# First product with w_out summed for four units at once in two of the ring's PSUM banks

## The chip, the cores and the metric

The kernel runs on one core of a Trainium2 chip. A core has TensorE for matrix products, VectorE, ScalarE and GpSimd for elementwise work, and SyncE, which issues most of the transfers. Every engine works through its own queue in order. The metric is the device time of one execution in microseconds; the median of three runs is compared. Matrix products write to PSUM, which has eight banks; everything else lies in SBUF.

## The reference: delta rule attention, then a gated feed-forward layer

For each of 4 batches x 8 heads, with 768 positions of 48 features, a state matrix is carried along the sequence:

```
k_n = k / (norm(k) + 1e-6)
for t in range(S):
    y[t] = q[t] @ state
    v_old = kn[t] @ state
    state += b[t] * outer(kn[t], v[t] - v_old)
```

The results, 3072 rows of 384 features, go through `h = x @ w_in` (384 x 2048), `g = h * sigmoid(1.702 h)` and `g @ w_out` (2048 x 384). All products are in 32-bit floats. The two weight matrices come as 64-bit floats and are converted on the chip.

## The kernel before

**Units.** The sequence is cut into 6 chunks of 128 positions. A unit is one chunk of one batch, so there are 24 units, four per chunk; two neighbouring units share a column block of x^T (`xT`, 256 tokens). Inside a unit the recurrence becomes a triangular system, solved in four blocks of 32 positions: `solve` multiplies by a block's inverse (into `psU`), `below` takes the solved block out of the later ones (into `psR`), `solved` copies psU on ScalarE, `rest` subtracts psR from V on VectorE. `scores` makes psQ (queries against keys and state, in two halves of two banks each), `queries` and `outputs` make psY (outputs) and the new state.

**Steps.** `woven(n, share)` is one step of the main part, from n = 3 on. It works on unit n-1 (its last blocks and its output), n and n+1 together, in three stages; in each it calls `together` (psU and psR) and then hands out pieces of the feed-forward layer with `spend`, so that TensorE has something to do while other engines evacuate. A step gets a share of 13.0 us for n up to 6 and 20.8 after that. `STEPS` tells how many operations of the next inversion (`invert`, VectorE) each stage gets; two steps share an inversion, begun at the odd one (5, 7, ...).

**The queue.** `queue` holds generators; each yield is a piece of 1.3 us. `hidden` makes gelu(x @ w_in) (tiles `gT`), `written` makes g @ w_out of two units, one after the other. For the first chunk's first two units stands `both_written`, which goes feature block by feature block (16 blocks f of 128 features, in the list `order`) and adds up both units in the two banks of ps_moe; the two other units follow by `written`. `follow` appends the next pair's two generators in every second step. What is left at the end runs without cover.

**Weights.** `fetch_in` and `fetch_out` bring raw 64-bit words, `conversion` turns them into 32-bit floats by five operations on VectorE and one on ScalarE. `conversions` puts the pieces in a row, so that a `fill(k)` anywhere issues the next k substeps; five substeps make one piece. w_out's raw words lie partly in rows of w_out that are not yet converted (`inside`: the first row) and partly in borrowed buffers (`outside`: the name of the borrowed tile). `fetches` tells which transfer is started when a piece is done. Transfers of the first eight entries of `order` go by GpSimd's queue, the others by SyncE's.

**Order.** Operations that go through `vec`, `act`, `pe`, `pool`, `sync` and `other_queue` keep the order in which the program issues them on their engine (their line is the helper's, 102); a plain `nc.sync.dma_start` may be moved by the scheduler (lines 87, 95, 554, 724, 768).

**Buffers.** PSUM: ps_big 2 banks, ps_seq 4 ("the ring": psU, psR, half of psQ, psY), ps_moe 2 (ph, po). In SBUF the tag gT has 8 buffers, which `spare` also lends to other uses; the tags M, xT have 3, and `o` (the rows of the result, and `last`, a part of the outputs that two units share) has 2.

**Keys.** `normalize_mixed` scales a unit's keys: the square on ScalarE, the sum on VectorE, the power on GpSimd, then reciprocal and product on VectorE. A step calls it for a later unit.

Of the kernel before, what the change touches and what calls it, by code (L numbers as in the profile page):

```python
# [8 lines left out]
F32 = mybir.dt.float32  # L9
I32 = mybir.dt.int32  # L10
# [4 lines left out]
PSUM = bass.MemoryType.PSUM  # L15
# [3 lines left out]
def kernel(  # L19
# [21 lines left out]
    B, H, S, D = q.shape  # L41
    DM, DFF = moe_w_in.shape
    C = 128
    NC = S // C
    NBH = B * H
    NP = H // 2
    DP = 64
    KC = DM // 128
    FC = DFF // 128
    BS = 32  # L50
    NB = C // BS
    HB = 2
    NTH = HB * C
    FQ = 4
# [12 lines left out]
    io = ctx.enter_context(tc.tile_pool(name="io", bufs=3))  # L67
    wk = ctx.enter_context(tc.tile_pool(name="wk", bufs=2))
    ps_big = ctx.enter_context(tc.tile_pool(name="ps_big", bufs=2, space=PSUM))
    ps_seq = ctx.enter_context(tc.tile_pool(name="ps_seq", bufs=4, space=PSUM))  # L70
    ps_moe = ctx.enter_context(tc.tile_pool(name="ps_moe", bufs=2, space=PSUM))
    dram = ctx.enter_context(tc.tile_pool(name="dram", bufs=2, space=bass.MemoryType.DRAM))

# [10 lines left out]
    def load(n, pairs, dma=nc.sync.dma_start):  # L84
        c, b = units[n]
        for dst, src in pairs:
            dma(  # L87
                out=dst[n % len(dst)][:, :, 0:D],
                in_=src[b, :, c * C : (c + 1) * C, :].rearrange("h p d -> p h d"),
            )  # L90
# [9 lines left out]
    def pinned(op):  # L100

        return lambda *a, **kw: tc.keep_in_program_order(op(*a, **kw))  # L102

    class Engine:

# [75 lines left out]
                )  # L181

    places, slots = {}, {}
    inside = {3: 6, 4: 8, 5: 10, 6: 12, 7: 14, 12: 14, 13: 10}
    outside = {0: "xT", 8: "xT", 11: "xT", 1: "M", 9: "M", 14: "M", 2: "M2", 10: "M2", 15: "M2"}
    order = [0, 1, 2, 3, 4, 5, 6, 7, 8, 13, 9, 10, 12, 11, 14, 15]

    def fetch_out(f):

        if f in outside:  # L190
            slot = outside[f]
            if slot not in slots:
                slots[slot] = wk.tile([128, 2 * DM], I32, tag=slot[:2].strip("2"), name="raw", bufs=3)
            words = slots[slot]
        else:
            words = raws[:, inside[f] * DM : (inside[f] + 2) * DM]
        places[f] = as_raw(words, (1, DM))
        first = order.index(f) < FC // 2
        (other_queue if first else sync)(
            out=as_rows(places[f])[:, 0], in_=moe_w_out[f * 128 : (f + 1) * 128, :]  # L200
        )
# [51 lines left out]
    def conversions():  # L253
# [27 lines left out]
    fetches = {  # L281
        ("in", 0, 1): lambda: fetch_in(3),
        ("in", 3, 1): lambda: fetch_out(3),
        ("out", 4): lambda: fetch_out(13),
        ("out", 6): lambda: fetch_out(12),
    }
    for new, old in ((8, 0), (9, 1), (10, 2), (11, 8), (14, 9), (15, 10)):
        fetches[("out", old)] = lambda f=new: fetch_out(f)
    converting = conversions()

    def fill(n):
        for _ in range(n):
            next(converting, None)
# [142 lines left out]
    def spare(name):  # L436
        t = wk.tile([128, FQ, NTH], F32, tag="gT", name=name, bufs=GB)
        return t.rearrange("p f t -> p (f t)")
# [118 lines left out]


    def bank(name, shape=(128, H, D)):
        return ps_seq.tile(list(shape), F32, tag="seq", name=name)  # L560

    lasts = [None]

    class Step:
# [19 lines left out]
        def scores(self):  # L584

            c, S = self.c, slice(128, 128 + D)
            self.QS = (
                spare("QS")[:, 0 : NP * (128 + D)].rearrange("p (j t) -> p j t", j=NP) if self.n == B - 1
                else wk.tile([128, NP, 128 + D], F32, tag="QS", name="QS", bufs=3)
            )  # L590
            transposed(self.qp, self.QS[:, :, 0:128])
            if c > 0:
                St = ST[:, self.b, 0 : NP * D].rearrange("p (j d) -> p j d", j=NP)
                act.activation(self.QS[:, :, S], St, ACT.Copy)
            yield
            self.M = (
                spare("M").rearrange("p (h t) -> p h t", h=H) if self.n in (B - 1, B + 1)
                else wk.tile([128, H, 128], F32, tag="M", name="M", bufs=3)
            )
            n = 128 + D if c > 0 else 128  # L600
            for g in range(0, NP, 2):
                pool_, tag = (ps_seq, "seq") if g else (ps_big, "big")
                ps = [pool_.tile([128, 2, 128 + D], F32, tag=tag, name="psQ") for _ in range(2)]
                for i in range(2):
                    for hh in range(2):
                        r = self.rows(hh)
                        pe.matmul(
                            ps[hh][:, i, 0:n], lhsT=self.kT[r, g + i, :],
                            rhs=self.QS[r, g + i, 0:n], start=True, stop=True,
                        )  # L610
                for hh in range(2):
                    hs = slice(2 * g + hh, 2 * g + 4, 2)
                    if c > 0:
                        Vh = self.V[:, hs, :]
                        vec.tensor_tensor(Vh, Vh, ps[hh][:, :, S], op=ALU.subtract)
                    copy = act.copy if hh == 0 or self.n < 2 * B + HB else vec.tensor_copy
                    copy(self.M[:, hs, :], ps[hh][:, :, 0:128])
                if g == 0:
                    yield
            if self.n >= B:  # L620
                self.select()
# [146 lines left out]
            nc.sync.dma_start(out=out[b * S + c * C : b * S + (c + 1) * C, :], in_=o)  # L768
            yield 1.3

    def both_written(c, gT):

        po = [ps_moe.tile([128, DM], F32, tag="moe", name="po") for _ in range(HB)]
        for n, f in enumerate(order):
            ahead = order[min(n + 3, FC - 1)]
            while ("out", ahead - ahead % 2 if 4 <= ahead < 8 else ahead) not in done:
                fill(1)
            for i in range(HB):
                pe.matmul(
                    po[i], lhsT=gT[f // FQ][:, f % FQ, i * C : (i + 1) * C], rhs=w_out[:, f, :],  # L780
                    start=(n == 0), stop=(n == FC - 1),
                )
            if n < FC - 1:
                yield 1.3
        for i in range(HB):
            o = wk.tile([128, DM], F32, tag="o", name="o")
            act.copy(o, po[i])
            sync(out=out[i * S + c * C : i * S + (c + 1) * C, :], in_=o)
        yield 1.3
# [15 lines left out]
    def ahead_of(work, n):  # L805
        for _ in range(n):
            next(work, None)
# [57 lines left out]
            debt[0] -= done  # L865

    STEPS = (9, 5, 3, 3, 3, 3)
    begun = {}

    def woven(n, share):  # L870

        nonlocal inverting
        A, B_, D_ = steps.pop(n - 1, None), steps.get(n), steps.get(n + 1) or NoStep()
        m = n + B + 1
        if n < B + HB:
            K = normalize_mixed(m + 1) if n <= B else iter(())
        else:  # L880
            K = (normalize if n > 6 else normalize_mixed)(m) if m < len(units) else iter(())
        P = prepare(m) if m < len(units) else iter(())
        if m in begun:
            P = begun.pop(m)
        if n % HB == 1 and B < n and n + 1 + HB < len(units):
            inverting = invert(*units[n + 1 + HB], HB)
        ahead = STEPS[:3] if n % HB == 1 else STEPS[3:]

        next(K, None)
        together([(B_, 1)], [(A, 2)])  # L890
        run(D_.scored)
        next(K, None)
        ahead_of(inverting, ahead[0])
        spend(share / 3)

        together([(A, 3), (D_, 0)], [(B_, 1)])
        next(K, None)
        ahead_of(inverting, ahead[1])
        spend(share / 6)
        next(P, None)  # L900
        spend(share / 6)

        together([(B_, 2)], [(D_, 0)])
        if A:
            A.queries()
            A.outputs()
        run(P)
        ahead_of(inverting, ahead[2])
        if n % HB == 0:
            run(inverting)  # L910
        spend(share / 6)
        next(new_step(n + 2).scored, None)
        spend(share / 6)
        follow(n)
# [38 lines left out]
    late_U = room[:, 0 : H * D + XR]  # L953
    pool.memset(late_U[:, H * D :], 0.0)
    zs = room[:, 512 : 512 + 6 * B * H].rearrange("p (s b h) -> p s b h", s=6, b=B)
    psD = [ps_seq.tile([128, B, NP, BS], F32, tag="seq", name="psD") for _ in range(2)]
    warm(NW)
    for b in range(B):
        squares_first(b)
# [133 lines left out]
    load(B + 2, ((QP, q),), sync)  # L1093
    for n in range(2 * B + 1, 2 * B + 1 + HB):
        load(n, ((KN, k),), sync)
    for i in range(22):
        ahead_of(inverting, 1)
        if i < 18:
            feed()
        if i in (2, 3, 4, 7, 8, 9, 10):  # L1100
            fetch_out(i - 2 if i < 5 else i - 3)
    run(inverting)
    def beside_conversion(work):
        for cost in work:
            fill(2)
            yield cost

    queue = [beside_conversion(w) for w in ffn] + [both_written(0, gTs[0]), written(*units[HB], gTs[1])]
    for n in range(B - 1, len(units) + 1):
        woven(n, 20.8 if n > 6 else 13.0)  # L1110
    run(take(1e9))
# [31 lines left out]
```

## Time and profile before

| | before |
|---|---|
| median of 3 runs | 772.58 us (771.7 to 773.25) |
| the profiled execution | 771.55 us, of that 769.8 us span |
| mean granted clock of TensorE | 0.977 |
| TensorE po matmuls | 768, 263.4 us busy |
| TensorE ph matmuls | 1152, 261.2 us busy |
| VectorE busy | 439.8 us |
| output rows: issue to landing | 2.0 us, median of 24 |
| w_out raw words on SyncE, issue to landing | 3.1 and 3.4 us |

"Busy" is time in which an engine executes an instruction. A matmul row counts one instruction; a product of 32-bit floats takes two of them. The number after "idle before" is what the engine waited ahead of the instruction, with the one whose end released it. The granted clock is the share of full speed that TensorE was given. Transfers are listed by their issue; when they land is listed apart.

### The profile page before, as it was taken

What the parts mean: (1) busy time and instruction counts of PE and PEld (TensorE: products, weight loads), DVE (VectorE), ACT (ScalarE), POOL (GpSimd) and SP (SyncE); (2) the same over time, 40 slices, a digit from 0 to 9 for tenths busy, and PEclk for the clock granted to TensorE, in tenths of its full rate; (3) what the DMA queues carried; (4) which work ended last, traced back from release to release, by engine and by line L of the source; (5) the groups of instructions that cost most, each with busy time, mean ns of one, the idle gap of its engine ahead of it and who ended that gap; (6) DMA issues with size and microseconds to landing.
All of it is one profiled execution on the core that took longest, in us unless ns stands there. A gap on an engine that the chain in (4) does not pass through costs nothing.

```text
span 769.8 us, 19471 instructions
## 1 busy us (share of the span) xinstructions
PE 743.6 (97%) x8508; PEld 558.0 (72%) x8508; DVE 439.8 (57%) x896; ACT 240.1 (31%) x535; POOL 128.4 (17%) x133
## 2 busy tenths in 40 slices
PE   7888999888999999999999999999999999999997
PEld 6666788556687687687688678678678677686774
DVE  5999897996766566566566566565566521000000
ACT  4567523343233233133133133124123132121110
POOL 6133301100222122122131121220210000000000
PEclk8599999989999999999999999999999999999999
DMA  9965355543142142142142142142030020000000
GB/s 158 173 121 114 86 146 124 141 107 82 40 96 57 37 93 56 37 95 56 35 96 57 34 97 56 25 107 57 22 81 9 24 42 2 17 11 1 26 1 21
DMA packets 131637, 50.78 MB, mean 66 GB/s; under 512 B 106432, under 2 KB 127040, under 8 KB 131552
## 3 DMA queue, kind: packets, MB, share of 16 engines
q1 hardware_dynamic: 129152, 41.27, 24.9%
q0 software_dynamic: 2400, 8.26, 4.4%
q8 instruction: 67, 1.10, 0.6%
q14 instruction: 18, 0.15, 0.1%
HBM read 32.08 MB, written 16.25 MB: 63 GB/s over the span
## 4 chain that ended last, share of the span: by engine, by line
PE 83%; DVE 8%; SPq 4%; issue 1%; ACT 1%; DMA 1%; POOL 0%; DVEq 0%; ACTq 0%
PE ph L102 32%; PE po L102 30%; PE psY L102 6%; PE psU L102 5%; SPq L102 4%; PE psQ L102 3%; PE psR L102 3%; PE psG L102 2%; DVE w_out L102 2%; PE psT L102 2%; DVE tmp L102 2%; DVE P L102 1%; DVE V L102 1%; DVE w_in L102 1%; DMA w_out<-in_moe_w_in_dram 1%
## 5 line engine op out<-in xcount | busy, mean ns | idle before, releaser
L102 PE MATMUL po<-w_out,gT 128*128 128x384 f32 x768 | 263.4, 494 | 3.3 <-DVE w_out L102 3.3
L102 PE MATMUL ph<-xT,w_in 128*128 128x256 f32 x1152 | 261.2, 383 | 0.3
L102 PEld LDWEIGHTS ph<-xT,w_in 128*128 128x128 f32 x1152 | 214.8, 190 | 32.5 <-issue 1.7
L102 PEld LDWEIGHTS po<-w_out,gT 128*128 128x128 f32 x768 | 142.2, 191 | 96.3 <-DVE w_out L102 4.2
L102 DVE TENSOR_TENSOR V<-V,psR 128x384 f32<-128x384 f32 (+2 forms) x72 | 40.1, 557 | 191.6 <-PE psR L102 191.0
L102 ACT ACTIVATE gT<-ph 128x512 f32<-128x512 f32 x96 | 56.5, 596 | 150.8 <-PE ph L102 150.7
L102 DVE TENSOR_TENSOR P<-NT,YB 64x8 f32<-64x8 f32 (+26 forms) x178 | 85.2, 479 | 4.7
L102 ACT COPY US<-psU 32x384 f32<-32x384 f32 x92 | 43.2, 470 | 139.6 <-PE psR L102 75.5
L102 PEld LDWEIGHTS psU<-V,XB 32*32 32x32 f32 x1536 | 58.3, 104 | 35.8 <-issue 25.6
L102 DVE TENSOR_REDUCE YB<-P 64x4 f32<-64x8 f32 (+27 forms) x178 | 77.2, 434 | 6.3 <-DVE P L102 0.2
L102 PE MATMUL psU<-V,XB 32*32 32x48 f32 x1536 | 69.5, 203 | 4.0 <-DVE V L102 3.9
L102 PE MATMUL psR<-US,G 32*32 32x48 f32 x2576 | 62.9, 204 | 1.0 <-issue 0.5
L624 POOL TENSOR_SCALAR_AFFINE_SELECT M<-M 128x1024 f32<-128x1024 f32 x20 | 25.1, 1253 | 220.9 <-DVE M L102 160.1
L102 PEld LDWEIGHTS psR<-US,G 32*32 32x32 f32 x2576 | 53.4, 104 | 2.0 <-issue 1.0
L102 PE MATMUL psQ<-QS,kT 48*128 48x176 f32 (+1 forms) x384 | 39.1, 350 | 5.4 <-ACT QS L102 5.4
L102 PEld LDWEIGHTS psQ<-QS,kT 48*128 48x128 f32 x384 | 32.1, 215 | 9.0 <-ACT QS L102 7.2
L102 DVE TENSOR_TENSOR P<-NT 64x256 f32<-64x256 f32 (+7 forms) x44 | 36.3, 825 | 0.3
L102 DVE TENSOR_REDUCE NT<-P 64x64 f32<-64x1024 f32 (+7 forms) x44 | 35.4, 803 | 1.5
L102 PE MATMUL psG<-kT 48*128 48x128 f32 x384 | 32.1, 304 | 1.9 <-ACT G L102 1.2
L102 ACT COPY o<-po 128x384 f32<-128x384 f32 x24 | 11.5, 479 | 71.5 <-issue 41.0
L87 POOL DMA_DIRECT2D KN<-in_k_dram x13 | 12.4, 953 | 116.1 <-PE psY L102 107.0
L102 ACT COPY M<-psQ 128x256 f32<-128x256 f32 x68 | 22.9, 377 | 24.8 <-DVE V L102 17.5
(102 smaller groups left out, 609.7 us busy)
## 6 DMA issues: line engine op xcount, KB each, us to landing
Nd<-G SPq DMA_DIRECT2D x16, 512.0 KB, 3.5
QP<-in_q_dram SPq DMA_DIRECT2D x24, 192.0 KB, 3.9
V<-in_v_dram SPq DMA_DIRECT2D x24, 192.0 KB, 3.3
out_dram<-o SPq DMA_DIRECT2D x24, 192.0 KB, 2.0
KN<-in_k_dram POOLq DMA_DIRECT2D x14, 192.0 KB, 3.8
NT<-Nd SPq DMA_DIRECT2D x20, 128.0 KB, 2.6
Yd<-YS SPq DMA_DIRECT2D x20, 128.0 KB, 2.5
XB<-Yd SPq DMA_DIRECT2D x20, 128.0 KB, 3.0
```

The costliest lines, as they stand in the source:

```text
L87: dma(out=dst[n % len(dst)][:, :, 0:D], in_=src[b, :, c * C : (c + 1) * C, :].rearrange("h p d -> p h d"),)
L102: return lambda *a, **kw: tc.keep_in_program_order(op(*a, **kw))
L624: (pool if self.n < B else nc.gpsimd).affine_select(out=self.M, in_=self.M, compare_op=ALU.is_gt, fill=0.0, base=0, pattern=[[0, H], [1, 1 ...
```

## The change

Four things are edited.

- `both_written` becomes `all_written`: the first chunk's four units are summed feature block by feature block. Two units stay in ps_moe's banks, two take two of the ring's four banks; the ring is split into two pools of two banks, and while the sums last (`turns[1]`) `seq` gives out only the first pool. Each half of a feature block is a piece, followed by 2 or 3 conversion substeps. The four output rows are copied out one after the other at the end and sent with the ordered `sync`.
- `order`, `inside`, `outside` and `fetches`: w_out's blocks come in another order, and the last parts' raw words lie elsewhere; blocks 9 and 11 use two gT buffers, fetched after block 7 has been multiplied. Unit 5's M goes to the pool M instead of a gT buffer.
- `SOON` replaces `STEPS` up to step 6: the inversion of steps 5 and 6 gets (0, 4, 6) and (5, 5, 5) operations in place of (9, 5, 3) and (3, 3, 3).
- Key 9's square is issued ahead of the main part, at turn 14 of the loop before it, and `beside_conversion` issues 3 substeps per piece in place of 2 once w_in is converted.

```diff
--- before.py
+++ after.py
@@ -67,7 +67,7 @@
     io = ctx.enter_context(tc.tile_pool(name="io", bufs=3))
     wk = ctx.enter_context(tc.tile_pool(name="wk", bufs=2))
     ps_big = ctx.enter_context(tc.tile_pool(name="ps_big", bufs=2, space=PSUM))
-    ps_seq = ctx.enter_context(tc.tile_pool(name="ps_seq", bufs=4, space=PSUM))
+    ps_seq = [ctx.enter_context(tc.tile_pool(name=f"ps_seq{i}", bufs=2, space=PSUM)) for i in range(2)]
     ps_moe = ctx.enter_context(tc.tile_pool(name="ps_moe", bufs=2, space=PSUM))
     dram = ctx.enter_context(tc.tile_pool(name="dram", bufs=2, space=bass.MemoryType.DRAM))
 
@@ -100,6 +100,14 @@
     def pinned(op):
 
         return lambda *a, **kw: tc.keep_in_program_order(op(*a, **kw))
+
+    turns = [0, False]
+
+    def seq(shape, name):
+
+        if not turns[1]:
+            turns[0] ^= 1
+        return ps_seq[0 if turns[1] else turns[0]].tile(list(shape), F32, tag="seq", name=name)
 
     class Engine:
 
@@ -181,15 +189,17 @@
                 )
 
     places, slots = {}, {}
-    inside = {3: 6, 4: 8, 5: 10, 6: 12, 7: 14, 12: 14, 13: 10}
-    outside = {0: "xT", 8: "xT", 11: "xT", 1: "M", 9: "M", 14: "M", 2: "M2", 10: "M2", 15: "M2"}
-    order = [0, 1, 2, 3, 4, 5, 6, 7, 8, 13, 9, 10, 12, 11, 14, 15]
+    inside = {3: 6, 4: 8, 5: 10, 6: 12, 7: 14, 15: 8, 12: 10, 14: 12, 8: 10}
+    outside = {0: "xT", 13: "xT", 10: "xT", 1: "M", 2: "M2", 9: "gT", 11: "gT2"}
+    order = [0, 1, 3, 4, 5, 6, 7, 2, 14, 15, 12, 13, 8, 9, 10, 11]
 
     def fetch_out(f):
 
         if f in outside:
             slot = outside[f]
-            if slot not in slots:
+            if slot not in slots and slot[:2] == "gT":
+                slots[slot] = spare("raw").bitcast(I32)[:, 0 : 2 * DM]
+            elif slot not in slots:
                 slots[slot] = wk.tile([128, 2 * DM], I32, tag=slot[:2].strip("2"), name="raw", bufs=3)
             words = slots[slot]
         else:
@@ -281,10 +291,9 @@
     fetches = {
         ("in", 0, 1): lambda: fetch_in(3),
         ("in", 3, 1): lambda: fetch_out(3),
-        ("out", 4): lambda: fetch_out(13),
-        ("out", 6): lambda: fetch_out(12),
+        ("out", 4): lambda: (fetch_out(15), fetch_out(12)),
     }
-    for new, old in ((8, 0), (9, 1), (10, 2), (11, 8), (14, 9), (15, 10)):
+    for new, old in ((13, 0), (14, 6), (8, 12), (10, 13)):
         fetches[("out", old)] = lambda f=new: fetch_out(f)
     converting = conversions()
 
@@ -557,7 +566,7 @@
 
 
     def bank(name, shape=(128, H, D)):
-        return ps_seq.tile(list(shape), F32, tag="seq", name=name)
+        return seq(shape, name)
 
     lasts = [None]
 
@@ -594,13 +603,16 @@
                 act.activation(self.QS[:, :, S], St, ACT.Copy)
             yield
             self.M = (
-                spare("M").rearrange("p (h t) -> p h t", h=H) if self.n in (B - 1, B + 1)
+                spare("M").rearrange("p (h t) -> p h t", h=H) if self.n == B - 1
                 else wk.tile([128, H, 128], F32, tag="M", name="M", bufs=3)
             )
             n = 128 + D if c > 0 else 128
             for g in range(0, NP, 2):
-                pool_, tag = (ps_seq, "seq") if g else (ps_big, "big")
-                ps = [pool_.tile([128, 2, 128 + D], F32, tag=tag, name="psQ") for _ in range(2)]
+                shape = [128, 2, 128 + D]
+                ps = [
+                    seq(shape, "psQ") if g else ps_big.tile(shape, F32, tag="big", name="psQ")
+                    for _ in range(2)
+                ]
                 for i in range(2):
                     for hh in range(2):
                         r = self.rows(hh)
@@ -768,21 +780,30 @@
             nc.sync.dma_start(out=out[b * S + c * C : b * S + (c + 1) * C, :], in_=o)
             yield 1.3
 
-    def both_written(c, gT):
-
-        po = [ps_moe.tile([128, DM], F32, tag="moe", name="po") for _ in range(HB)]
+    def all_written(c, gTs):
+
+        turns[1] = True
+        po = [
+            (ps_moe if i < HB else ps_seq[1]).tile([128, DM], F32, tag="moe" if i < HB else "seq", name="po")
+            for i in range(B)
+        ]
         for n, f in enumerate(order):
-            ahead = order[min(n + 3, FC - 1)]
+            ahead = order[min(n + 2, FC - 1)]
             while ("out", ahead - ahead % 2 if 4 <= ahead < 8 else ahead) not in done:
                 fill(1)
-            for i in range(HB):
+            for i in range(B):
                 pe.matmul(
-                    po[i], lhsT=gT[f // FQ][:, f % FQ, i * C : (i + 1) * C], rhs=w_out[:, f, :],
-                    start=(n == 0), stop=(n == FC - 1),
+                    po[i], lhsT=gTs[i // HB][f // FQ][:, f % FQ, i % HB * C : (i % HB + 1) * C],
+                    rhs=w_out[:, f, :], start=(n == 0), stop=(n == FC - 1),
                 )
-            if n < FC - 1:
-                yield 1.3
-        for i in range(HB):
+                if i % HB == HB - 1 and (n < FC - 1 or i < B - 1):
+                    fill(2 + i // HB)
+                    yield 1.3
+            if f == 7:
+                fetch_out(9)
+                fetch_out(11)
+        turns[1] = False
+        for i in range(B):
             o = wk.tile([128, DM], F32, tag="o", name="o")
             act.copy(o, po[i])
             sync(out=out[i * S + c * C : i * S + (c + 1) * C, :], in_=o)
@@ -865,7 +886,8 @@
             debt[0] -= done
 
     STEPS = (9, 5, 3, 3, 3, 3)
-    begun = {}
+    SOON = (0, 4, 6, 5, 5, 5)
+    begun, squared = {}, {}
 
     def woven(n, share):
 
@@ -875,7 +897,9 @@
         nonlocal inverting
         A, B_, D_ = steps.pop(n - 1, None), steps.get(n), steps.get(n + 1) or NoStep()
         m = n + B + 1
-        if n < B + HB:
+        if m + 1 in squared:
+            K = squared.pop(m + 1)
+        elif n < B + HB:
             K = normalize_mixed(m + 1) if n <= B else iter(())
         else:
             K = (normalize if n > 6 else normalize_mixed)(m) if m < len(units) else iter(())
@@ -884,9 +908,11 @@
             P = begun.pop(m)
         if n % HB == 1 and B < n and n + 1 + HB < len(units):
             inverting = invert(*units[n + 1 + HB], HB)
-        ahead = STEPS[:3] if n % HB == 1 else STEPS[3:]
-
-        next(K, None)
+        ahead = SOON if n < B + HB + 1 else STEPS
+        ahead = ahead[:3] if n % HB == 1 else ahead[3:]
+
+        if n != B - 1:
+            next(K, None)
         together([(B_, 1)], [(A, 2)])
         run(D_.scored)
         next(K, None)
@@ -953,7 +979,7 @@
     late_U = room[:, 0 : H * D + XR]
     pool.memset(late_U[:, H * D :], 0.0)
     zs = room[:, 512 : 512 + 6 * B * H].rearrange("p (s b h) -> p s b h", s=6, b=B)
-    psD = [ps_seq.tile([128, B, NP, BS], F32, tag="seq", name="psD") for _ in range(2)]
+    psD = [seq((128, B, NP, BS), "psD") for _ in range(2)]
     warm(NW)
     for b in range(B):
         squares_first(b)
@@ -1093,8 +1119,11 @@
     load(B + 2, ((QP, q),), sync)
     for n in range(2 * B + 1, 2 * B + 1 + HB):
         load(n, ((KN, k),), sync)
+    squared[2 * B + 1] = normalize_mixed(2 * B + 1)
     for i in range(22):
         ahead_of(inverting, 1)
+        if i == 14:
+            next(squared[2 * B + 1])
         if i < 18:
             feed()
         if i in (2, 3, 4, 7, 8, 9, 10):
@@ -1102,10 +1131,10 @@
     run(inverting)
     def beside_conversion(work):
         for cost in work:
-            fill(2)
+            fill(3 if ("in", 3, 1) in done else 2)
             yield cost
 
-    queue = [beside_conversion(w) for w in ffn] + [both_written(0, gTs[0]), written(*units[HB], gTs[1])]
+    queue = [beside_conversion(w) for w in ffn] + [all_written(0, gTs)]
     for n in range(B - 1, len(units) + 1):
         woven(n, 20.8 if n > 6 else 13.0)
     run(take(1e9))
```

## The prediction, made before the result was known

> **What bounds the kernel now.** I read the page's shares and slices first, then TensorE's and VectorE's timelines from 95 to 236 us, two-microsecond windows for the granted clock, and SyncE's queue. Stretches below are by the span. "Step n" is one call of woven; each has three stages, and a "piece" is one yield of the queue (1.3 us of TensorE: six ph or four po instructions). The page:
>
> ```profile
> PE 743.6 (97%) x8508; PEld 558.0 (72%) x8508; DVE 439.8 (57%) x896; ACT 240.1 (31%) x535; POOL 128.4 (17%) x133
> ...
> PE   7888999888999999999999999999999999999997
> ...
> PEclk8599999989999999999999999999999999999999
> ```
>
> TensorE is the bound from about 180 us on: its idle time lies in the first ten slices, so the matmuls after that are a fixed amount, and the end moves by what TensorE loses or regains before. The place in question is steps 4 and 5. TensorE's timeline there, with the idle time in brackets:
>
> ```profile
> 148.96 1.56 PE L102 MATMUL po<-w_out,gT 128*128 128x384 f32 x4 [1.15 <-DVE w_out L102]
> ...
> 155.04 1.16 PE L102 MATMUL psG<-kT 48*128 48x128 f32 x16 [0.62 <-ACT kT L102]
> ...
> 160.06 0.66 PE L102 MATMUL psT<-ident,QP 128*128 128x128 f32 x4 [1.08 <-ACT G L102]
> ...
> 164.65 2.72 PE L102 MATMUL psQ<-QS,kT 48*128 48x176 f32 x16 [1.85 <-ACT QS L102]
> 167.30 6.06 PE L102 MATMUL po<-w_out,gT 128*128 128x384 f32 x12
> 175.50 1.56 PE L102 MATMUL po<-w_out,gT 128*128 128x384 f32 x4 [2.13 <-DVE w_out L102]
> ```
>
> The same stretch in windows (length; busy time of TensorE, weight loads, VectorE, ScalarE, GpSimd; clock; DMA):
>
> ```profile
> 162.00:164.00 2.00, 0.81 (x33) 0.67 (x32) 1.93 (x6) 0.75 (x2) 0.00 (x0) 1.00 1.02 248
> 164.00:166.00 2.00, 1.35 (x10) 1.35 (x12) 1.93 (x6) 1.16 (x3) 0.00 (x0) 0.60 0.18 39
> 166.00:168.00 2.00, 2.00 (x11) 1.42 (x10) 1.94 (x7) 1.15 (x5) 0.00 (x0) 0.50 0.83 141
> ```
>
> VectorE has no idle moment there (1.93 of 2.00 is issue to issue): one single feature of w_out costs it 2.2 us (starts 154.83 to 157.03), a pair 3.9. TensorE catches up with it, and after the third gap its clock is halved. VectorE's lag shows in one row: the psR matmuls end at 162.80, their subtraction starts only at 166.50, 3.70 later.
>
> ```profile
> 166.50 0.56 DVE L102 TENSOR_TENSOR V<-V,psR 32x384 f32<-32x384 f32 x1
> ```
>
> SyncE's queue at the end of step 6 is the other place:
>
> ```profile
> 213.50 0.98 SPq L768 DMA_DIRECT2D out_dram<-o  x1
> 215.50 0.33 SPq L102 DMA_DIRECT2D NT<-Nd  x1
> 215.92 1.96 SPq L102 DMA_DIRECT2D Yd<-YS  x2
> 219.63 1.00 SPq L102 DMA_DIRECT2D XB<-Yd  x2
> ```
>
> It waits for Nd, then for Yd to land, and whatever stands behind waits too. Line 102 marks what keeps its order; line 768 does not, and so the old output row could slip ahead of NT.
>
> **The change part by part.** *Same work.* The queue hands out 40 pieces in steps 3 to 6 (4 x 13.0 / 1.3): eight of ph, 32 of po before and after. The 64 pairs of feature and unit stay; only their order changes. So no matmul is gained.
>
> *The conversions spread out, -11.05.* Before, 16 features must be ready within 16 pieces, now within 32. Substeps of conversion issued: by the end of step 4 before 111 of 115, after 92; the last ones leave at the end of step 5. Step 4 then holds some 25 substeps (about 13 us of VectorE) instead of 40 (20). The gaps at steps 4 and 5 that this can take away are 0.76 (psQ, 140.18) + 1.15 + 0.62 + 1.08 + 1.85 + 2.13 = 7.59; the half clock cost 2.66 - 1.39 for psQ and 6.06 - 3.87 for the po x12, 3.46. Together 11.05, which I take; less is possible, since what covered VectorE's old work now also covers the subtractions.
>
> *Key 9's square sooner: 0 by itself.* VectorE idles 2.52 us before its ssq at 122.79; the sum follows YS directly, and GpSimd's power too. It speeds conversions up at step 3, where TensorE runs on ph; the gain is inside the 11.05. ScalarE's square (0.51) moves in between the gelu tiles, before each of which ScalarE waits about 2 us.
>
> *Raw words elsewhere: 0 to 8 on VectorE, little on TensorE.* Fetch 14 starts when the pair 6, 7 is done, and its first conversion follows two substeps later (0.86 us) while a w_out fetch on SyncE lands after 3.1 to 3.4: VectorE waits some 2.6. Fetch 8 after 12 has the same shape. 9 and 11 need gT buffers that are free only after feature 7's matmuls; 9's first substep is issued one piece later (1.3 us): some 2.5. All this goes into the lag below. Step 5's M goes back to its own pool; ScalarE's 1.2 us wait for po goes, off the path.
>
> *Inversion later (SOON): 0 as such.* Ten of 25 operations in step 5 instead of 17, 15 in step 6 instead of 8 and the end. By the rows at 179 to 213 that puts 4.7, 7.9 and 7.9 us of VectorE work into step 6's stages, whose TensorE time is 7.6, 5.9 and 8.6. What is late next is the subtraction of step 6's third stage, behind 7.9 us.
>
> *Two banks fewer in the ring until all four sums are done: +9.3.* psU and psR of a stage now hold both banks; psQ's second half (stage 1) and psY (stage 3) must wait for ScalarE's copy and VectorE's subtraction. With four, psY starts at 205.17, right behind psR. At best each wait is the subtraction, 0.56 and a signal; psQ's first half (0.70, other banks) covers it, psY's two (steps 5, 6) stand bare: 1.2. At worst, following VectorE's queue, psG waits 1.5 in step 4 (ScalarE's kT copy stands behind a conversion's Relu), psY 3.5 in step 5, psQ 1.9 and psY 4.6 in step 6: 11.5. I take the measured lag of 3.70 for both psY and 1.9 for the psQ: 9.3, nearer the upper end because the lag row is from this very place.
>
> *The four output rows at the end of step 6: +10.3.* This is the step that decides. The o tiles have two buffers, one held by `last`. The copies of po 0 and 1 fill both; the copy of po 2 needs the first row's transfer finished. That transfer is now ordered on SyncE, behind NT, Yd and XB of units 8 and 9, which are issued before it. Step 7 begins with psU and psR, of which one takes a bank of the second pool, and both are held by po 2 and 3. TensorE stands, with the whole of step 7 behind it; ScalarE too, in order. From the end of step 6's psY: Yd issues 8.67 later (207.25 to 215.92, set by xT, Nd and NT), XB 3.71 after that, two XB issues 1.00, the output lands after 2.0, copy 0.48: 15.86. TensorE needs only 5.60 for that stretch (207.25 to 212.85). So it stands 10.3; 11.5 if YS itself comes late by SOON. Were the row not behind XB: QS copies 0.93, copy 0.48, landing 2.0, copy 0.48 less the last piece's 1.29: 2.6.
>
> *The clock after it: +3.3.* The window at 10:12 has TensorE busy 0.19 of 2.00, and from 15 us the clock is 0.50. After the gaps around 163 it is halved for 6.6 us, which costs 3.3. A stall of 10 should do the same: 0 (none follows) to 6.6 (also after step 6's psY).
>
> The Trainium skill, "TensorE: Matmul & The Clock Gate", section "What's actually happening", has the gate close after an idle window of about 3.4 us and open after one busy window. By that rule an estimate is 1.7 us after step 7 in place of 3.3, and 783 as the time. The trace differs: 1.85 idle after 0.62 and 1.08 was enough here, while 2.13 at 173.4 left the clock at 1.00.
>
> Against the change speaks "Perfetto Trace Analysis", section "Matmuls": independent groups should rotate through different banks so that evacuation overlaps the next group. It has no price.
>
> Sum against the profiled execution's 771.55 (span 769.8): -11.05 + 9.3 + 10.3 + 3.3 = +11.9, 783.4; the median of the runs, 772.58, is 1.0 higher: 784.
>
> **The rivals.** (1) Faster: the first output row gets out before the XB pair, or its buffer is free earlier, so step 7 stands only 2.6. Then -11.05 + 2.6 leaves 8.4 for the bank waits: below that the kernel is faster, above slower. With 1.2 to 9.3 of waits it is -7.2 to +0.9: 765 to 773, middle 769. For it: the old row did slip ahead at 213.50. Against: that one was not ordered, these are.
>
> (2) The change does all that it says: VectorE keeps up, waits are hidden under psQ and the copies do not hold step 7. -11.05 + 1.2 + 1, about 764. For it: VectorE has idle time from 176 on (2.54, 1.50, 1.45). Against: the banks of po 2 and 3 have to be copied out before step 7 in any order.
>
> (3) Raw words come late: the three waits of about 2.6 on VectorE reach po itself, while step 7 is held by 2.6: -11.05 + 9.3 + 2.6 + 7.8 = +8.7, 781. Against: matmuls trail their conversions by about four features.
>
> **How the numbers follow.** Forecast 0.66, 784, own range 773 (waits 1.2, no slow clock: +0.5) to 791 (waits 11.5, stall 11.5, clock 6.6: +18.6). Rival 1 0.16, rival 2 0.08, rival 3 0.10. Range 767 to 791: below lie rival 2 and a third of rival 1, above a part of the forecast's own upper end. A measurement tells from no change what exceeds about 0.2%, 1.5 us. Faster: rival 2 and three quarters of rival 1, 0.20; same 0.04; slower 0.76.
>
> **What would show it.** Right: in step 7 psU or psR starts more than 8 us after the last po of feature 11, with o<-po on ScalarE just ahead of it and XB, then out_dram, on SyncE; psY of steps 5 and 6 with an idle bracket of 0.6 to 4.6; no gap at po from w_out; granted clock below 1 after step 7's gap. Wrong: out_dram ahead of Yd; psY directly behind psR; step 6 beginning later than 190.86, which would mean that the conversions did not release the gaps.

## The result and the profile after

The changed kernel takes 791.54 us (median of four runs, 790.21 to 793.15) against 772.91 for the kernel before, run beside it: a ratio of 1.0242, 95% interval 1.0212 to 1.0271. The forecast was 784 with a range up to 791; the sign and the places are right, the size is 7.5 us short. The profiled execution took 790.37, of that a span of 788.7: 18.9 us more than before.

The page of the changed kernel, in the same three lines: the work of TensorE is the same (8508 instructions), its share of the span is not, and a hole stands in the twelfth slice of 20 us.

```profile
PE 750.0 (95%) x8508; PEld 564.0 (72%) x8508; DVE 438.9 (56%) x896; ACT 240.1 (30%) x535; POOL 128.9 (16%) x133
...
PE   7888999979849999999999999999999999999997
...
PEclk7599999998969999999999999999999999999999
```

TensorE's timeline of the changed kernel from 138 to 230 us, the instructions with idle time ahead of them (the small ones under 0.5 us are left out but for the first; it is the only gap left in step 4):

```profile
152.75 1.16 PE L102 MATMUL psG<-kT 48*128 48x128 f32 x16 [0.40 <-ACT kT L102]
...
177.06 1.68 PE L102 MATMUL psY<-QS,ST 48*64 48x128 f32 x16 [4.74 <-DVE V L102]
...
190.27 0.86 PE L102 MATMUL psQ<-QS,kT 48*128 48x176 f32 x6 [1.17 <-DVE V L102]
...
208.96 1.12 PE L102 MATMUL psY<-QS,ST 48*64 48x128 f32 x14 [3.15 <-DVE V L102]
...
228.44 0.28 PE L102 MATMUL psU<-V,XB 32*32 32x48 f32 x1 [10.16 <-ACT o L102]
```

No po waits for w_out any more: the conversions are ahead. In their place stand the two psY (of steps 5 and 6), half a psQ, and psU of step 7, which waits for ScalarE's copy of an output row. ScalarE's and SyncE's timelines say why. ScalarE copies the third and fourth row only when an output transfer has landed:

```profile
227.91 0.97 ACT L102 COPY o<-po 128x384 f32<-128x384 f32 x2 [8.88 <-DMA out_dram<-o]
```

and that transfer left SyncE's queue last:

```profile
220.85 0.33 SPq L102 DMA_DIRECT2D NT<-Nd  x1
222.12 0.80 SPq L102 DMA_DIRECT2D Yd<-YS  x2
224.09 1.04 SPq L102 DMA_DIRECT2D XB<-Yd  x2
225.22 4.02 SPq L102 DMA_DIRECT2D out_dram<-o  x4
```

VectorE's lag ahead of psY of step 5 has a source of its own: twice it stands for raw words of w_out (blocks 8 and 9).

```profile
163.90 0.36 DVE L102 TENSOR_SCALAR w_out<-w_out 128x384 int32<-128x384 int32 x1 [2.34 <-DMA w_out<-in_moe_w_out_dram]
...
168.81 0.36 DVE L102 TENSOR_SCALAR w_out<-raw 128x384 int32<-128x384 int32 x1 [2.62 <-DMA raw<-in_moe_w_out_dram]
```

The four steps, by the start of psU in TensorE's timeline:

| start of | before | after | difference |
|---|---|---|---|
| step 4 | 138.56 | 138.39 | -0.2 |
| step 5 | 161.94 | 158.35 | -3.6 |
| step 6 | 190.86 | 187.11 | -3.8 |
| step 7 | 212.84 | 228.44 | +15.6 |
| step 7, second stage | 223.00 | 242.33 | +19.3 |

Step 4 is 3.4 us shorter, step 5 gives back all that it gains, step 6 with the wait after it loses 19.4, and the first stage of step 7 takes 13.9 instead of 10.2 though it does the same work. That last figure is the clock. Windows of the changed kernel (the columns as in the prediction; the last three are granted clock, DMA share and GB/s), one from each of four spells at half clock:

```profile
178.00:180.00 2.00, 2.00 (x26) 1.67 (x20) 0.00 (x0) 0.00 (x0) 0.00 (x0) 0.50 0.03 8
192.00:194.00 2.00, 2.00 (x4) 1.04 (x4) 1.86 (x5) 0.00 (x0) 2.00 (x2) 0.50 0.03 8
210.00:212.00 2.00, 2.00 (x25) 1.99 (x24) 0.00 (x0) 0.00 (x0) 0.00 (x0) 0.50 0.00 0
232.00:234.00 2.00, 2.00 (x8) 1.34 (x7) 1.35 (x4) 1.08 (x4) 0.31 (x1) 0.50 0.02 9
```

Each spell follows one of the four waits. Half of TensorE's busy time in them is lost: 2.3 us at 177 to 182, 1.7 at 192 to 195, 1.7 at 209 to 212, 3.9 at 228 to 236, together 9.6.

### The profile page after: what moved, and what is told of

Read it like the earlier page. It is cut to its first block, busy times and chain, and to the rows that moved or that the text cites. A ratio compares the mean times of both kernels' runs of the same rounds, so it can differ in the third digit from the quotient of the medians.

```text
span 788.7 us, 19470 instructions
## 1 busy us (share of the span) xinstructions
PE 750.0 (95%) x8508; PEld 564.0 (72%) x8508; DVE 438.9 (56%) x896; ACT 240.1 (30%) x535; POOL 128.9 (16%) x133
## 4 chain that ended last, share of the span: by engine, by line
PE 85%; DVE 8%; DMA 3%; ACT 2%; issue 1%; SPq 0%; DVEq 0%; ACTq 0%
PE ph L102 31%; PE po L102 29%; PE psY L102 6%; PE psU L102 5%; PE psQ L102 5%; PE psG L102 4%; PE psR L102 2%; PE psT L102 2%; DVE P L102 2%; DVE YB L102 1%; PE ps_warm L102 1%; DVE w_out L102 1%; DMA w_out<-in_moe_w_out_dram 1%; DVE tmp L102 1%; DVE V L102 1%
## 5 line engine op out<-in xcount | busy, mean ns | idle before, releaser
L102 PE MATMUL psU<-V,XB 32*32 32x48 f32 x1536 | 70.2, 204 | 13.5 <-ACT o L102 10.2
```

## The experiments

The theory after the result: the loss has two sources and a price on top of both. SyncE's order holds step 7 through the two o buffers; VectorE's lag, made worse by late raw words and the later inversion, holds psY through the ring's two banks; and such a wait is paid a second time by the clock. The rivals: that step 7 waits for the inversion itself, that two banks are too few whatever VectorE does, and that the clock falls for another reason. All ratios are to the kernel before, run beside each.

**Output rows in four buffers of their own.** The transfers keep their place in SyncE's queue; only the buffer is no longer what the copies wait for.

```diff
-            o = wk.tile([128, DM], F32, tag="o", name="o")
+            o = spare("o")[:, 0:DM]
             act.copy(o, po[i])
```

> Changed kernel, but the four output rows of all_written lie in four buffers of gT (free since feature 2) instead of the two of tag o. Theory (step 7 is held by the buffer behind the out transfer behind XB): the 10.16 us wait of psU at step 7 shrinks to about 1.1 (QS copies 0.93, three copies 1.44, less the last piece 1.29), and the half clock after it (about 3.9 us) goes: 791.5 - 9.1 - 3.9 = 778 to 779. Rival (step 7 waits for XB itself or for VectorE's late YS): psU still starts after 225 us, time 788 or more. The two psY waits (4.7 and 3.6) stay under both.

Measured: 780.24 us, ratio 1.0055 (1.0031 to 1.0080); the profiled span is 775.5, 13.2 less than the changed kernel's. The two psY waits are as they were (4.88 and 3.15); step 7's is 0.78:

```profile
208.96 1.12 PE L102 MATMUL psY<-QS,ST 48*64 48x128 f32 x14 [3.15 <-DVE V L102]
...
218.98 0.23 PE L102 MATMUL psU<-V,XB 32*32 32x48 f32 x1 [0.78 <-ACT o L102]
```

The clock is 1.00 from 214 us on. So 13.2 us of the profiled span hang on two buffers (11.3 by the medians): 9.4 of wait and 3.8 of clock. Neither XB's landing nor the inversion holds step 7.

**Free order of the four output transfers.**

```diff
-            sync(out=out[i * S + c * C : i * S + (c + 1) * C, :], in_=o)
+            nc.sync.dma_start(out=out[i * S + c * C : i * S + (c + 1) * C, :], in_=o)
```

> Changed kernel, but the four out transfers of all_written are plain, so that the scheduler may move them: in the instruction order the first stands ahead of NT, the second between Yd and XB, the third and fourth behind one XB each. Theory: copy 3 follows the first transfer by 2.4 us, so psU starts about 3 us after the last po instead of 10; then psQ waits for copy 4, which waits for the second transfer behind Yd, 3 to 4 us more. TensorE still stands for some 6 to 8 us in two parts: 786 to 790. Rival (the order of the out transfers is of no account, XB's chain itself holds step 7): wait of 10 as before, 791.

Measured: 789.87 us, ratio 1.0174 (1.0128 to 1.0220), within what was expected. psU waits 2.78 and psQ 2.64, both for a copy into o: the first row goes out early, the second still stands behind Yd. Half of the wait goes, its half clock (228 to 235) stays, and little is won. The order is a cause, but a looser queue is not enough while there are two buffers.

**The old spread of the inversion.**

```diff
-    SOON = (0, 4, 6, 5, 5, 5)
+    SOON = STEPS
```

> Changed kernel with the old spread of the inversion (9, 5, 3; 3, 3, 3) in steps 5 and 6 instead of (0, 4, 6; 5, 5, 5). Theory: VectorE waits for raw words for 5 us in the first stage of step 5, so nine operations there cost little, and step 6 has 8 us less to do in its third stage: psY of step 6 waits 0.6 instead of 3.6, psQ of step 6 no longer 1.2, YS comes about 8 us sooner, and with it XB and the out transfers; step 7's wait is then set by xT, Nd and NT on SyncE and stays near 10. Gain 4 to 6 with its half clock (1.5): 785 to 788. Rival (the spread makes room for the conversions, so undoing it delays them): psY of step 5 waits longer than 4.7, time 791 or more.

Measured: 792.23 us, ratio 1.0217 (1.0172 to 1.0262): no gain, the rival's case. psY of step 6 did fall to 0.49 as the theory said, but the work went to step 5: there psU waits 3.97 and psY 6.30, psQ of step 6 waits 2.83. Nine operations in the first stage of step 5 were not covered by the waits for raw words. In time the two spreads cannot be told apart (1.0217 and 1.0242).

**Two banks of the ring alone.** The kernel before, `ps_seq` split as in the change, the second pool idle in steps 4 to 6:

```diff
     for n in range(B - 1, len(units) + 1):
+        turns[1] = B <= n < B + 3
         woven(n, 20.8 if n > 6 else 13.0)
```

> Kernel before, but psU, psR, psQ's second half and psY get only two of the ring's four banks in steps 4 to 6; two banks lie idle, and nothing else is changed. It prices the ring alone. Theory (a wait for a bank is as long as VectorE and ScalarE lag): psQ of step 4 about 2.4 (US copy at 143.3), psQ of step 5 about 1.0, psY 0.6 in steps 5 and 6, psQ of step 6 0.3, together 4 to 5, and 0 to 3.3 of half clock: 776 to 781. Rival (the ring is free as long as VectorE keeps up; only the late conversions made psY wait): 772.9 to 774.5.

Measured: 777.73 us, ratio 1.0037 (1.0006 to 1.0068); the median of the runs beside it is 774.18, so some 3 us (0.5 to 5.3 by the interval). The waits are where the theory puts them, with the sizes of the lag; after the first one the clock is 0.50 from 143 to 150 us, which the kernel before does not have there:

```profile
143.10 1.54 PE L102 MATMUL psQ<-QS,kT 48*128 48x176 f32 x6 [2.00 <-ACT US L102]
...
169.17 1.63 PE L102 MATMUL psQ<-QS,kT 48*128 48x176 f32 x8 [1.08 <-ACT US L102]
...
187.01 0.84 PE L102 MATMUL psY<-QS,ST 48*64 48x128 f32 x16 [0.49 <-ACT US L102]
```

Here the psY waits are 0.49, the bare evacuation, where the changed kernel has 4.74 and 3.6. The ring is a small price where VectorE keeps up.

**Key 9's square alone.** The kernel before with the square at turn 14.

```diff
+    squared[2 * B + 1] = normalize_mixed(2 * B + 1)
     for i in range(22):
         ahead_of(inverting, 1)
+        if i == 14:
+            next(squared[2 * B + 1])
```

> Kernel before with one part of the change alone: key 9's square is issued at turn 14 of the loop ahead of the main part. Theory: VectorE's 2.5 us wait for it at 120 us goes, the conversions run up to 2.5 us sooner in steps 3 and 4, and some of TensorE's gaps at 148 to 164 us shrink, until the inversion's and the scores' work fills them again: 0 to 2.5 us faster, 770 to 773. Rival (ScalarE's square delays the gelu tiles): no change or slower by 0.5.

Measured: 774.03 us, ratio 1.0018 (0.9995 to 1.0040): nothing that can be told from no change, at the slow edge of what was expected. The gaps from 148 to 165 us are the same to 0.01 us (1.15, 0.62, 1.08, 1.85). The time that VectorE wins at 120 us is gone by the next wait for TensorE (4.20 us at 133.60, in place of 1.59). But after the same gaps the clock stays at 1.00 here, and then po waits longer for w_out:

```profile
175.40 2.93 PE L102 MATMUL po<-w_out,gT 128*128 128x384 f32 x4 [5.47 <-DVE w_out L102]
```

In the kernel before it waits 2.13 and starts at 175.50. So the half clock at 164 to 171 cost the kernel before nothing by itself: TensorE would have stood for VectorE's conversions instead. Here the half clock follows that wait (174 to 180), and the profiled execution is 2.3 us longer.

**Raw words earlier.** A first try put block 12's conversion into rows that still held raw words of block 14, so that block 14's values there are not the reference's; its instructions and transfers are those named.

```diff
-    inside = {3: 6, 4: 8, 5: 10, 6: 12, 7: 14, 15: 8, 12: 10, 14: 12, 8: 10}
-    outside = {0: "xT", 13: "xT", 10: "xT", 1: "M", 2: "M2", 9: "gT", 11: "gT2"}
-    order = [0, 1, 3, 4, 5, 6, 7, 2, 14, 15, 12, 13, 8, 9, 10, 11]
+    inside = {3: 6, 4: 8, 5: 10, 6: 12, 7: 14, 15: 10, 12: 8, 14: 12, 8: 10}
+    outside = {0: "xT", 13: "xT", 10: "xT", 1: "M", 2: "M2", 9: "xT2", 11: "gT"}
+    order = [0, 1, 3, 4, 5, 6, 7, 2, 15, 14, 12, 13, 8, 9, 10, 11]
```

> Changed kernel, but no raw words come late: 9 uses a third buffer of tag xT and is fetched when 1 is done, 8 is fetched when 15 is done (15 and 12 change places in memory, 15 and 14 in the order), 11 alone waits for feature 7. Theory (psY of step 5 waits 4.7 because VectorE stood for raw words for 2.3 and 2.6 us before): that wait falls to 0.5 to 1.5, its half clock (2.3) goes, step 6's and 7's waits stay: 784 to 787. Rival (VectorE is late by sheer work): psY of step 5 still waits 4 or more, 790 or more.

Measured: 786.27 us, ratio 1.0169 (1.0138 to 1.0200). VectorE waits for no raw words in step 5, and psY of step 5 waits 1.27; step 7's wait is 10.91. Repeated without that clash (order as in the change, 9 and 11 in "xT2" and "xT3", fetched after 1 and 2):

> Changed kernel with the early raw words alone, without the clash of the first try. Theory: VectorE no longer waits for raw words in step 5; psY of step 5 waits 1 to 2 instead of 4.7; step 6's waits (1.2, 3.6) and step 7's (10) stay: 785 to 787, as in the first try. Rival: the first try's gain came from its other order, 790 or more.

Measured: 787.78 us, ratio 1.0199 (1.0182 to 1.0217), 3.8 us less than the changed kernel; psY of step 5 waits 2.87 instead of 4.74, more than expected. But this run does not do all that its theory says. Block 9's wait is gone; block 8's is not, because its fetch still leaves SyncE behind NT, at 160.37 (in the changed kernel at 160.49). VectorE's timeline and SyncE's:

```profile
164.35 0.36 DVE L102 TENSOR_SCALAR w_out<-w_out 128x384 int32<-128x384 int32 x1 [3.20 <-DMA w_out<-in_moe_w_out_dram]
```

```profile
159.93 0.34 SPq L102 DMA_DIRECT2D NT<-Nd  x1
160.37 0.52 SPq L102 DMA_DIRECT2D w_out<-in_moe_w_out_dram  x1
```

In the first try, with block 15 first, it left ahead of NT. There psY's wait fell by 3.5 us, so late raw words were the larger part of VectorE's lag in step 5; the order of the blocks differs too. With the first try's places and its clash, rows and raw words together:

> Both: output rows in gT buffers and early raw words. By the sum of the two: 780 less 5 to 7, 773 to 776; what is left against the kernel before are the waits of step 6 (psQ 1.2, psY 3.6) and their half clock, and the gain of the spread conversions, 11. Rival (the gain of 11 depended on the waits): 778 or more.

Measured: 774.23 us, ratio 1.0009 (0.9982 to 1.0036), as expected: with the two causes out, the kernel is level with the kernel before. And with another spread, `SOON = (6, 4, 4, 4, 3, 4)`:

> The same with the inversion of steps 5 and 6 spread by VectorE's room, (6, 4, 4; 4, 3, 4) in place of (0, 4, 6; 5, 5, 5). Theory: psY of step 6 waits 0.5 to 1 instead of 3.6, psQ of step 6 below 0.5, no half clock after step 4: 766 to 769, faster than both kernels. Rival: the six operations in the first stage of step 5 make psY of step 5 wait 3 to 4 again, 772 to 775.

Measured: 771.87 us, ratio 0.9991 (0.9974 to 1.0008): the rival's case. psY of step 6 waits 0.49, but psY of step 5 4.40. VectorE's timeline of that kernel: psR's subtraction of the second stage and that of the third, 5.9 us apart, and between them inversion and conversion without a gap:

```profile
169.42 0.56 DVE L102 TENSOR_TENSOR V<-V,psR 64x384 f32<-64x384 f32 x1
...
175.36 0.56 DVE L102 TENSOR_TENSOR V<-V,psR 128x384 f32<-128x384 f32 x1
```

**Work moved out of the second stages.** The mended raw words, the rows in gT, and:

```diff
-    SOON = (0, 4, 6, 5, 5, 5)
+    SOON = (4, 0, 8, 5, 2, 6)
...
-                    fill(2 + i // HB)
+                    fill(3)
```

> Changed kernel with output rows in gT buffers, early raw words without a clash (order as in the change; 9 and 11 in free buffers of tag xT, 8 after 15), three conversion substeps after every half feature, and the inversion spread (4, 0, 8; 5, 2, 6), so that VectorE has nothing but conversion rests in step 5's second stage and little in step 6's. Theory (what is left of the loss is VectorE's lag at the third stages): psY waits 0.5 to 1 in both steps, psQ of step 6 below 0.5, step 7 0.8, no half clock between 130 and 230 us: the gain of 11 less about 3, 763 to 766, faster than both kernels. Rival (VectorE's work up to step 6 is too much in any spread): one wait of 3 or more remains, 769 to 772.

Measured: 768.09 us against 773.45, ratio 0.9938 (0.9916 to 0.9960): faster than both kernels, though not by the 7 to 10 us that were expected. Its runs lie between 766.7 and 773.6; the profiled one took 771.03, with a mean clock of 0.977 where the quickest have 0.982. In that profile psY of step 5 waits 0.49 and 0.67, in two parts, and

```profile
203.73 0.84 PE L102 MATMUL psY<-QS,ST 48*64 48x128 f32 x16 [0.49 <-ACT US L102]
...
212.42 0.23 PE L102 MATMUL psU<-V,XB 32*32 32x48 f32 x1 [0.78 <-ACT o L102]
```

but a new wait of 1.96 stands in step 6 (psT for key 11, whose scaling on VectorE now comes behind the inversion of the first stage), and two half-clock spells, 177 to 181 and 198 to 201, remain. The first follows gaps of at most 0.67. That those spells are what parts its best runs from its others was not tested.

**A wait by itself.** The kernel before, in which TensorE waits for a chain of k dependent one-column copies on ScalarE at the start of four steps where the clock is 1.00:

```diff
+    def hold(k):
+        ps = ps_big.tile([128, NP, 128], F32, tag="big", name="psH")
+        pe.matmul(ps[:, 0, 0:1], lhsT=ident, rhs=table, start=True, stop=True)
+        act.activation(table, ps[:, 0, 0:1], ACT.Copy)
+        for _ in range(k):
+            act.activation(table, table, ACT.Copy)
+        pe.matmul(ps[:, 1, 0:1], lhsT=ident, rhs=table, start=True, stop=True)
+    HOLD = {9: 2, 11: 8, 13: 20, 15: 45}
```

> Kernel before, in which TensorE is made to wait at the start of steps 9, 11, 13 and 15 for a chain of 3, 9, 21 and 46 dependent one-column copies on ScalarE (about 0.2 us each: waits of some 0.6, 2, 4.5 and 10 us). It prices a wait by itself in a stretch where the clock is full. Theory (a wait of a few us costs a spell of half clock on top, 2 to 4 us each): the granted clock falls after the last two waits at least, and the time rises by 17 us of waits and 5 to 8 us of clock, 794 to 798. Rival (half clock comes from long low load, not from one wait): clock 1.00 throughout, 789 to 791.

Measured: 806.51 us, ratio 1.0436 (1.0411 to 1.0461); 33 us for waits of 1.04, 2.45, 5.26 and 11.12, 19.9 together. That is above both expectations. The windows after the first and around the second wait:

```profile
278.00:280.00 2.00, 1.76 (x42) 1.68 (x44) 0.50 (x1) 0.66 (x2) 0.00 (x0) 1.00 0.89 236
338.00:340.00 2.00, 0.32 (x3) 0.30 (x3) 0.00 (x0) 1.42 (x7) 0.00 (x0) 1.00 0.86 181
342.00:344.00 2.00, 2.00 (x13) 1.62 (x12) 1.06 (x5) 0.39 (x2) 0.00 (x0) 0.50 0.39 59
348.00:350.00 2.00, 2.00 (x11) 1.77 (x10) 1.72 (x9) 0.60 (x1) 0.29 (x1) 1.00 0.01 4
```

After 1.04 us the clock stays at 1.00; after 2.45 it is 0.50 from about 340.6 to 347.4, after 5.26 until 415.7, after 11.12 until 487.3. TensorE works at half speed for 6.8, 8.2 and 5.9 us of these: 3.4, 4.1 and 3.0 us, 10.5 in all. Between 2.45 and 11.12 the wait's length hardly matters for that loss. In the profiled execution what follows step 15's wait comes 31.7 us later than what stands ahead of step 9's, measured against the kernel before: 19.9 of waits, 10.5 of clock and 1.3 that is in neither.

**Keeping TensorE busy through step 7's wait.** The changed kernel with 76 idle products ahead of psU:

```diff
+        if n == 7:
+            ps = ps_big.tile([128, 256], F32, tag="big", name="ps_busy")
+            for _ in range(76):
+                pe.matmul(ps, lhsT=ones[:, 0:128], rhs=ones, start=True, stop=True)
```

> Changed kernel with 76 idle bf16 products (each about 0.12 us, 9.5 us in all) in a free bank ahead of step 7's psU: TensorE works through most of the 10.16 us for which it would stand, and psU can start no sooner than before (228.4 in the profile). It parts the wait from the clock. Theory (the half clock after step 7, 3.9 us, is a price of its own that idleness brings): clock 1.00 from 218 to 238 us and 3 to 4 us faster than the changed kernel, 787 to 788.5. Rival (the clock falls for another reason, such as the load of step 7's small products): same as the changed kernel, 791 to 792.

Measured: 789.22 us, ratio 1.0183 (1.0139 to 1.0228), between the two cases. The products took 8.46 us, not 9.5, and a wait of 2.38 was left; after it the clock was 0.50 from 229.5 to 236. So it did not part wait and clock as meant, and the two profiled spans are level (788.9 and 788.7). It does show that 2.38 us of idleness bring nearly the same spell as 10.16: step 7's first stage then takes 13.4 us, against 13.9 in the changed kernel and 10.2 in the kernel before.

## Why the prediction was right in sign and place, and short in size

- *The bound.* TensorE from 180 us on: right. Everything after step 7 shifts as one piece (19.3 us at step 7's second stage, 18.9 at the end).
- *The conversions' gain, -11.05.* Right: the gaps at po, QS and the half clock at 165 are gone. What is left of them is 0.40 at psG, so the gain is 10.65. The split into 7.59 of gaps and 3.46 of clock is not firm: in the run with key 9's square alone the clock stayed full there, and the same gaps came to 10.9.
- *Same work.* Right: 8508 instructions in both.
- *Key 9's square at 0.* Right within the noise, by its own run.
- *The ring, +9.3.* The size is right: 4.74 + 1.17 + 0.49 + 3.15 = 9.55, at places that were named. By part it is less good: psY of step 5 waited 1.0 more than I took and psQ 0.7 less, which cancels in part. Its source was named right too (lag, raw words, the inversion's 7.9 us), but I called the ring the price; with VectorE in time it costs about 3.
- *The inversion "0 as such".* Misleading: the old spread takes 1.5 us of wait out of step 6 and puts 5.5 into step 5.
- *Step 7, +10.3.* Right: 10.16, with the order of SyncE as foretold. That the size fits so well is luck: Yd came 0.8 us later than I took, held not by NT but by YS, which VectorE ended at 222.10; the output landed 0.7 later; and XB was issued 1.7 sooner. Rival 1's price of 2.6 was right for psU when the first row did leave early (2.78 with the free order), but it left out the second row's wait at psQ (2.64).
- *The clock, +3.3.* **This is the step that failed.** I charged one spell, after step 7, and up to two in the range. There were four, 9.6 us: after step 5's psY, step 6's psQ and psY, and step 7. That is 6.3 us more than I took, of the 7.5 that are missing. The terms with their measured sizes give -10.65 + 9.55 + 10.16 + 9.6 = 18.7, of 18.9. My own rows showed a spell after gaps of 1.85 and less; a wait of 3.7, which I took for both psY, had to be charged the same. Three spells at 3.3 would have put the forecast at about 791, and so the range had to reach higher. The fourth could not be foretold from its wait: after the same 1.17 at psQ the clock stayed at 1.00 with the free order of the output transfers and in the first try with early raw words.
- *The clock gate.* The Trainium skill, page "TensorE: Matmul & The Clock Gate", section "What's actually happening", has it close after at least one idle window of about 3.4 us and open after at least one busy window. Here waits of 2.38 and 2.45, shorter than such a window, closed it, and it stayed closed for 6.8 us after the second; the measurement decides.
- *Rotating through banks.* The Trainium skill, page "Perfetto Trace Analysis", section "Matmuls", advises that independent groups rotate through different banks. This case agrees: two banks in place of four cost some 3 us.

## What to carry to other kernels

Where a program fills TensorE to the brim, count a long wait twice: its length, and the half clock after it. In these profiles every wait of 2.78 us or more that began at full clock was followed by half clock, which cost 1.7 to 4.1 us where it was worked out above; of the shorter ones, down to 1 us, some were and some were not. A buffer's release is only as early as the last transfer that reads it, and that as early as what stands ahead of it in an ordered queue; look at who waits for the engine that waits. When accumulators take banks from a ring, the ring's price is the evacuating engine's lag, so first move that engine's other work away from the stages that evacuate.

## What the runs showed of the hardware that was not expected

After waits put in at full clock the half clock lasted 6 to 8 us of TensorE's work whether the wait was 2.45, 5.26 or 11.12 us; in the changed kernel the spells lasted 3.4 to 7.8. Below 2.78 us no length of wait decides: 2.13 us at 173 in the kernel before and 2.50 at 176 with two banks of the ring left the clock at 1.00, while in the changed kernel 1.17 us in step 6 was followed by a spell, and in two other runs the same 1.17 was not. What decides there stays open. Two runs of one kernel can differ by 4 us with mean clocks of 0.966 and 0.977, which is why small differences here need many runs.
